# Second attention layer: values two visits behind the scores and placed right after them, weight transfers placed behind the first q transfers, scalings of V reordered

## The chip, the cores and the metric

The kernel runs on one core of one Trainium2 chip. The metric is device time in microseconds (us) of one execution; lower is better. Names of engines: PE is the matrix engine (PEld its weight loads), ACT the scalar engine, DVE the vector engine, POOL the GpSimd engine, SP the engine that issues most DMA transfers. A product, below, is a group of four matmuls (128 rows by 128 columns of weights, 512 moving columns) that adds into one PSUM bank.

## What is computed

Four residual steps on one input of 2048 tokens by 1024 features, in bf16: attention layer A, token-mixing MLP B, and both once more with the same weights.

```python
def _A_ref(x, wqkv, wo):
    H = 32; Dh = D // H
    W, dil = 8, 2
    qkv = (x @ wqkv) ...               # q, k, v: 32 heads of 32 features
    idx = pos[:, None] - off[None, :]  # each token sees itself and 7 more, every second one back
    ...
    logits = jnp.einsum("bhsd,bhswd->bhsw", q, kg) * scale
    attn = _softmax(where(mask, logits, -1e9))
    o = jnp.einsum("bhsw,bhswd->bhsd", attn, vg)
    return o @ wo                      # heads joined again

x = x + _A_ref(_layernorm(x), A_wqkv, A_wo)
x = x + _B_ref(_layernorm(x), ...)     # layernorm, matmul over tokens, gelu, matmul over tokens
x = x + _A_ref(_layernorm(x), A_wqkv, A_wo)
x = x + _B_ref(_layernorm(x), ...)
```

## The kernel before

Tokens are kept in two classes (even and odd positions), since the window steps by two; each class has 1024 tokens, eight tiles of 128. The first attention layer computes q and k by plain matmuls and goes through 32 **visits**; a visit is one group of four heads, one class, one half of that class's tokens. In a visit the scores S (`scores_mm`, L779) are matmuls with 32 weight columns each (128*32 in the profile's rows); ACT takes the exponential (`expo`, L794, two instructions e.a and e.b), DVE multiplies it by a band mask into the buffer `Pm` (`mask_r`, L809, four instructions m.0 to m.3), and later the values V (`values_mm`, L820) multiply `Pm` by v, again with 32 weight columns each, into one accumulator bank pair. Two ACT instructions make the reciprocal of the sums (l, `recip_a` L853; x, `recip_b` L856), and DVE multiplies by it (n, `divide` L859). `Pm` has room for three visits; a V of an odd visit also reads the end of the visit before it.

The second attention layer, the one that the change touches, computes v, q and k by seven half-size products in place of eight (sums and differences of the quarters of weights and of data). Class `Sevens` (L412) does this for v: ACT scales the four weight tiles to fp16 (`scale`), DVE forms the sums of weights (`t_sum`) and of data (`s_sum`); the scalings and the first sums are placed in the last round (i = 7) of the MLP's second matmul, `gemm2f` (L1453, its round starts at L1668). Class `QkBlocks` (L501) loads the eight blocks of q and k weights (`load`, two transfers ahead), scales them on ACT, forms their sums on DVE and stores both to DRAM (`keep`, two transfers of 512 KB a block). Class `Attention` (L529) then runs nine **cycles**, numbered p = 0 to 8. Cycle p makes k and q of one head group of one class by two times seven products (P1k to P7k, P1q to P7q), and holds the four visits of the group before it: scores S1 to S4 and values V1 to V4, with e, m, l, x, n of the same numbers. Cycle 0 has only products, cycle 8 only what is left of the seventh. Weights come back from DRAM by `load(phi)` (L565): two transfers of 512 KB, named Aq and Bq, for k (even phi = 2p) and q (odd phi = 2p+1). A q that is ready lies in the buffer `qs`; it has to be spread over the heads in `qB`, which the scores read, by DMA: d c11q, d y12q, d y22q, d c21q, four transfers of 32 KB each (L658), and a few columns by DVE (`hq`, L664).

The order on each engine is written out by hand in four strings (L531 to L534); "-" means of the cycle before:

```python
PE = "P1k P4q- P5k S1 P6k V1 P2k P7k S2 P3k V2 P4k P1q P5q S3 P6q V3 P2q P3q S4 P7q V4"
ACT = "abk c21q- e1a e1b pck l1 x1 Zk e2a e2b c11k l2 x2 c21k abq e3a e3b pcq l3 c11q x3 Zq e4a e4b l4 x4"
DVE = "m10 m11 m12 m13 n1 y22k y12k m20 m21 m22 n2 m23 t1 t2 m30 m31 m32 m33 n3 y12q y22q hq m40 ..."
SP = "dc21q- wk wq dc11q dy12q dy22q"
```

ab and pc copy a partial sum to another bank (L693), Z scales one (L696), c11 and c21 (L700), y12 and y22 (L701) write a finished quarter of k or q; t1 and t2 are sums of data for the other class, in cycles 0 to 3. P6 waits for ab, P7 and P3 for pc, P4 for y22. `wk` and `wq` load the weights of cycle p+1's q (phi = 2p+3) and of cycle p+2's k (phi = 2p+4); in cycle 0 these are loads 3 and 4. Each engine takes its instructions strictly in this order, SP too. The V of a visit stands one visit behind its S. After the cycles, four last visits are interleaved with the first output projections (L1913).

The queue of SP around the start of the attention is, in order: stores of blocks 4 and 5, load 1, stores of blocks 6 and 7 (L1891), load 2 (L1894), load 3 and load 4 (cycle 0), then twelve q transfers of cycle 0, then cycle 1's.

Of the kernel before, what the change touches and what calls it, by code (L numbers as in the profile page):

```python
# [9 lines left out]
ACT = mybir.ActivationFunctionType  # L10
# [18 lines left out]
def kernel(  # L29
# [498 lines left out]

    class Attention:  # L529
        NP = 4 * NG // 4  # L530
        PE = "P1k P4q- P5k S1 P6k V1 P2k P7k S2 P3k V2 P4k P1q P5q S3 P6q V3 P2q P3q S4 P7q V4"  # L531
        ACT = "abk c21q- e1a e1b pck l1 x1 Zk e2a e2b c11k l2 x2 c21k abq e3a e3b pcq l3 c11q x3 Zq e4a e4b l4 x4"
        DVE = ("m10 m11 m12 m13 n1 y22k y12k m20 m21 m22 n2 m23 t1 t2 m30 m31 m32 m33 n3 y12q y22q hq m40 m41 m42 n4 m43")
        SP = "dc21q- wk wq dc11q dy12q dy22q"  # L534

        def __init__(self):
            self.T = {}
# [42 lines left out]
        def needs(self, n, p):  # L580
            k, f = n[:-1], n[-1]
            o, d = ("q", p - 1) if f == "k" else ("k", p)
            if n[0] == "d":
                return [(n[1:], p)]
            if n[0] == "w":
                return [("P4q", p - 1)] if f == "k" else [("P4k", p)]
            if n == "hq":
                return [("y12q", p)]
            if f in "kq":
                r = {"P1": [("c11" + o, d)], "ab": [("P1" + f, p), ("y12" + o, d)], "P5": [("Z" + o, d)],  # L590
                     "Z": [("P5" + f, p), ("y22" + o, d), ("y12" + o, d)], "P6": [("ab" + f, p)],
                     "pc": [("P6" + f, p), ("c21" + o, d)], "P2": [("ab" + f, p)], "P7": [("pc" + f, p)], "P3": [("pc" + f, p)],
                     "c11": [("P2" + f, p)], "y22": [("P7" + f, p), ("Z" + f, p)], "y12": [("P3" + f, p), ("Z" + f, p)],
                     "P4": [("y22" + f, p)], "c21": [("P4" + f, p)]}[k]
                if f == "q" and k in ("c11", "y12", "y22", "c21"):
                    r.append(("d" + n, p - 1))
                if f == "k" and k == "P1":
                    r.append(("wk", p - 2))
                return r
            if n[0] == "t":  # L600
                return [("P5q", p)] if p == 3 else []
            c = n[1]
            o, d = {"1": ("4", p - 1), "2": ("1", p), "3": ("2", p), "4": ("3", p)}[c]
            return {"S": [("e" + o + "a", d), ("e" + o + "b", d), ("dc11q", p - 1), ("dy12q", p - 1), ("hq", p - 1)]
                    + ([("dc21q", p - 1), ("dy22q", p - 1)] if c in "34" else []),
                    "e": [("S" + c, p)], "m": [("e" + c + "a", p), ("e" + c + "b", p)],
                    "V": [("m" + o + str(r), d) for r in range(4)] + [("l" + o, d), ("n" + o, d)],
                    "l": [("V" + c, p)], "x": [("l" + c, p)], "n": [("x" + c, p)]}[n[0]]

        def there(self, n, p):  # L610
            if p < 0 or n[-1] in "kq" and n[0] != "w" and p >= self.NP:
                return False
            if n[0] == "w":
                return p < self.NP
            if n[0] == "t":
                return (n, p) in self.extra
            if n[0] in "SemVlxn":
                return 1 <= p <= self.NP - 1 + (0 if n[0] in "SemVlxn" else 1) and not (p == 1 and n[0] in "Vlxn" and n[1] == "1")
            return True

        def cycle(self, p):
# [29 lines left out]
        def do(self, n, p):  # L651
# [9 lines left out]
            if n == "hq":  # L661
                for h in range(HG):
                    hp = slice(h * DH, (h + 1) * DH)
                    r = nc.vector.tensor_copy(out=qB[0][hp, h, 512:512 + W], in_=self.qs[hp, 1, 0:W])  # L664
                return r
            if n[0] == "w":
                phi = 2 * p + (3 if f == "k" else 4)
                if phi < 2 * self.NP:
                    self.load(phi)
                elif phi - 2 * self.NP < NDC:  # L670
                    self.load_wo(phi - 2 * self.NP)
                return
# [29 lines left out]
                                                      op0=ALU.mult, op1=ALU.add)  # L702
            if n[0] == "t":
                return self.extra[n, p]()
            vis = 4 * (p - 1) + int(n[1]) - 1 - (n[0] in "Vlxn")
            u, b = divmod(vis, 2)
            if n[0] == "S":
                mm, x["ss", vis] = scores_mm(u, b)
# [744 lines left out]
    def gemm2f(g, src, dst, seam):  # L1453
# [214 lines left out]
        for i in range(2, NI):  # L1668
# [20 lines left out]
            if i == 2:  # L1689
                chain_(A, move, Z[:], pd)  # L1690
                scaled(j, q[j][:, 0], 1, 1)
            else:
                if more:
                    scaled(j, q[j][:, 0], 1, 1)
                else:
                    sv[0].scale(0)
                chain_(A, move, Z[:], pd)
                if more:
                    scaled(j, q[j][:, 1], 0, 1)
                else:  # L1700
# [7 lines left out]
            if i == 5:  # L1708
                power_wv()
            if not more:  # L1710
                sv[0].scale(1)
                sv[0].scale(3)
                for n in range(4):
                    for m in range(2):
                        sv[0].s_sum(m, n)
# [14 lines left out]
            else:  # L1730
                seam(i + 2 - NI)
            if not more:
                for m in range(2):
                    sv[0].t_sum(3, m)
                    sv[0].t_sum(1, m)
# [22 lines left out]
            in_order(product, pc, weights(A22), [T4k(k) for k in range(K)], False)  # L1758
            prev = pc
        i = NI - 1  # L1760
        quarter(i, 1, 0, prev)
        aggregate(i, 1)
        for m in range(2):
# [5 lines left out]

        return rest  # L1770

    sv = [None]
    NU = NG * DIL
    hT, qB = new_hT(), new_qB()
    for li in range(2):
# [75 lines left out]
            chain_("DVE", power, 0, 1 + NPRE, bc0[:].rearrange("p q b -> p b q"))  # L1851
            ahead_tiles = 4
        else:
            blocks, at = QkBlocks(), Attention()

            def ahead(p, n):
                two_ = (p, p + 1)
                if n == 0:
                    if p == 0:
                        rest()  # L1860
                        chain_("POOL", zero_p, nc.gpsimd)
                    elif p == 2:
                        chain_("POOL", zero_q, nc.gpsimd)
                    if p:
                        blocks.keep(p - 2)
                        blocks.keep(p - 1)
                    if p == 4:
                        at.load(0)
                elif n == 2:
                    for k in two_:  # L1870
                        blocks.scale(k)
                    if p == 6:
                        at.load(1)
                else:
                    if p + 2 < NI:
                        for m in range(4):
                            for k in range(2):
                                sv[0].s_sum(p + 2 + k, m)
                        for k in range(2):
                            blocks.load(p + 2 + k)  # L1880
                    for j in range(2):
                        for m in {2: (3,), 4: (1,), 6: (2, 4)}.get(p, ()):
                            chain_("DVE", at.t_sum, 0, m, j)
                    for k in two_:
                        blocks.sums(k)

            for k in range(2):
                blocks.load(k)
            sv[0].run(v, ahead)
            for k in range(2):  # L1890
# [12 lines left out]
            ahead_tiles = 7  # L1903
            plan = [1, 2, 2, 1, 1]
            k = 0
# [85 lines left out]
```

## Time and profile before

| | us |
|---|---|
| time of three runs, median (lowest, highest) | 1210.99 (1208.9, 1212.31) |
| profiled execution: its own time | 1207.65 |
| profiled execution: span from the first to the last instruction | 1205.6 |
| PE busy (99% of the span) | 1188.8 |
| DVE busy (67%) | 805.6 |
| ACT busy (61%) | 734.6 |
| last round of `gemm2f` on PE | 586.98 to 609.16 |
| `Sevens.run`, v | 609.16 to 658.04 |
| cycles 0 to 8 of the second attention | 658.04 to 798.67 |

Times in the trace count from the first instruction. A line of the timeline gives start, length, engine, line of the code, operation, what is written and read, shape, count, and in brackets the engine's idle time before it with what ended that. Since matmuls overlap in the array, the distance between two starts, not the length, is what a product costs: 0.863 us from one product to the next.

### The profile page before, as it was taken

The page shows a single profiled execution, that of the slowest core. Times are in us where ns is not written, and L with a number is a line of the kernel's source. Part 1 is how long each engine was busy: PE and PEld are TensorE (multiplying, and loading weights), DVE is VectorE, ACT ScalarE, POOL GpSimd, SP SyncE. Part 2 cuts the span into 40 slices and gives each one's busy share as a digit, 9 for nine tenths or more (in the row PEclk, how much of TensorE's full clock was granted, in tenths as well). Part 3 has the DMA queues.
Part 4 walks back from the last instruction along what each step waited for, and adds up shares of the span by engine and source line. Part 5 has one row for each costly group of instructions (what it writes and reads, how often), then busy time and mean ns, then how long its engine had stood idle before and what let it go on. Part 6 is the DMA issues. An engine that isn't in the chain of part 4 may idle for free.

```text
span 1205.6 us, 20706 instructions
## 1 busy us (share of the span) xinstructions
PE 1188.8 (99%) x7908; PEld 540.3 (45%) x7908; DVE 805.6 (67%) x1541; ACT 734.6 (61%) x1220; POOL 138.3 (11%) x124
## 2 busy tenths in 40 slices
PE   9999999999999999999999899999999999999998
PEld 4444444444444444444444344444444444444444
DVE  6558887887777546866678488789633422784663
ACT  4767876678878776665668488865443434432342
POOL 0000000281000041000040000002811212100000
PEclk9999999999999999999999899999999999999999
DMA  8922233696675778876468634544867755165520
GB/s 241 152 63 71 77 110 92 210 280 168 203 211 171 205 197 193 226 179 162 127 201 283 233 116 166 192 123 155 285 195 207 226 163 158 53 192 140 149 80 36
DMA packets 258739, 201.53 MB, mean 167 GB/s; under 512 B 50256, under 2 KB 228816, under 8 KB 255312
## 3 DMA queue, kind: packets, MB, share of 16 engines
q1 hardware_dynamic: 258640, 200.21, 57.6%
q8 instruction: 62, 1.02, 0.4%
q14 instruction: 37, 0.30, 0.1%
HBM read 147.07 MB, written 38.82 MB: 154 GB/s over the span
## 4 chain that ended last, share of the span: by engine, by line
PE 87%; DMA 4%; DVE 3%; ACT 3%; issue 1%; SPq 1%; DVEq 0%; ACTq 0%
PE s L1142 11%; PE m L750 9%; PE m L900 7%; PE m L1142 7%; PE s L1351 7%; PE a L1142 6%; PE s L1501 4%; PE m L1351 4%; PE m L642 4%; PE s L299 3%; PE a L1351 3%; PE m L1501 3%; PE s L642 3%; PE s L981 2%; PE s L1594 2%; PE s L787 2%
## 5 line engine op out<-in xcount | busy, mean ns | idle before, releaser
L811 DVE TENSOR_TENSOR Pm<-pc,band 32x640 bf16<-32x640 bf16 x256 | 124.2, 485 | 41.7 <-ACT pc L795 35.5
L1142 PEld LDWEIGHTS <-Sw 128*128 128x128 f16 x832 | 81.4, 98 | 98.9 <-issue 0.9
L750 PE MATMUL m<-hT,wqk 128*128 128x512 bf16 x512 | 115.9, 380 | 0.0
L900 PE MATMUL m<-wo,oT 128*128 128x512 bf16 x512 | 112.9, 379 | 1.2 <-DVE xn L907 1.1
L1142 PEld LDWEIGHTS <-w 128*128 128x128 f16 (+1 forms) x624 | 61.0, 98 | 73.6
L900 PEld LDWEIGHTS <-oT 128*128 128x128 bf16 x512 | 49.4, 98 | 61.8 <-issue 4.0
L795 ACT ACTIVATE pc<-s,shift 128x320 bf16<-128x320 f32 x128 | 60.7, 528 | 26.6 <-PE s L787 26.6
L750 PEld LDWEIGHTS <-wqk 128*128 128x128 bf16 x512 | 47.6, 98 | 59.0 <-issue 5.3
L995 POOL TENSOR_TENSOR T<-h 128x512 f16<-128x512 bf16 x16 | 18.4, 1153 | 442.6 <-ACT h L940 442.6
L995 DVE TENSOR_TENSOR py<-pz,m 128x512 f32<-128x512 f32 x14 | 9.6, 688 | 86.7 <-PE m L1142 64.7
L1142 PE MATMUL s<-T,Sw 128*128 128x512 f16 x288 | 66.2, 379 | 0.6 <-ACT s L1151 0.6
L995 POOL TENSOR_TENSOR Pm<-g 128x512 f16<-128x512 bf16 x24 | 28.6, 1210 | 286.0 <-ACT Pm L1076 163.9
L940 ACT ACTIVATE h<-xn,bi,rs 128x1024 bf16<-128x1024 bf16 x32 | 39.7, 1240 | 23.6 <-DVE bi L926 23.6
L1142 PE MATMUL m<-T,Sw 128*128 128x512 f16 x224 | 52.9, 379 | 0.0
L1142 PE MATMUL a<-h,w 128*128 128x512 bf16 x224 | 52.9, 379 | 0.0
L1118 ACT ACTIVATE w<-w,cs 128x2048 f16<-128x2048 bf16 x26 | 51.8, 1997 | 0.0
L907 DVE TENSOR_TENSOR xn<-m,xr 128x512 bf16<-128x512 f32 x64 | 43.9, 685 | 11.0 <-PE m L900 10.7
L1351 PEld LDWEIGHTS <-u 128*128 128x128 f16 x336 | 32.9, 98 | 39.6
L995 DVE TENSOR_TENSOR xs<-tq,xs 128x512 bf16<-128x512 f32 (+1 forms) x30 | 21.9, 731 | 42.7 <-ACT tq L1506 25.6
L862 DVE TENSOR_TENSOR oT<-a,rd 128x512 bf16<-128x512 f32 x64 | 44.2, 691 | 8.5 <-ACT rd L857 6.6
L1108 DVE TENSOR_REDUCE mx<-w 128x1 f32<-128x2048 bf16 x22 | 49.2, 2276 | 0.0
L995 DVE TENSOR_TENSOR py<-pz,s 128x512 f32<-128x512 f32 x12 | 8.3, 688 | 55.6 <-PE s L1142 46.6
(286 smaller groups left out, 2440.8 us busy)
## 6 DMA issues: line engine op xcount, KB each, us to landing
w<-in_B_w_dram SPq DMA_DIRECT2D x110, 512.0 KB, 6.0
sd<-Sw SPq DMA_DIRECT2D x13, 1024.0 KB, 7.9
Sw<-sd SPq DMA_DIRECT2D x13, 1024.0 KB, 5.1
xa<-xn SPq DMA_DIRECT2D x32, 256.0 KB, 4.0
xs<-xa SPq DMA_DIRECT2D x32, 256.0 KB, 3.3
Aq<-sdq SPq DMA_DIRECT2D x16, 512.0 KB, 6.0
Bq<-sdq SPq DMA_DIRECT2D x16, 512.0 KB, 4.7
Pm<-in_B_w_dram SPq DMA_DIRECT2D x26, 256.0 KB, 6.2
```

Source lines behind the costliest of these rows:

```text
L642: r = nc.tensor.matmul(out, lhsT=lhs[:, k, :], rhs=rhs[:, k, :], start=start and k == 0, stop=k == 3, skip_group_check=True)
L750: mm = nc.tensor.matmul(ps[:], lhsT=wts[part][:, kt, (g % 2) * P:(g % 2 + 1) * P], rhs=hT[:, kt, lo:lo + 512], start=(kt == 0), stop=(kt = ...
L795: return nc.scalar.activation(out=pc[:, 2 * n:2 * n + 2].rearrange("p t h k -> p (t h k)"), in_=ss[n][:, 0:2 * HG * GW], func=ACT.Exp, sca ...
L811: return nc.vector.tensor_tensor(out=Pm[rp, :, s0:s0 + HB, r * KG:r * KG + GW].rearrange("p h t k -> p t h k"), in0=pc[rp], in1=mk, op=ALU ...
L862: return nc.vector.tensor_tensor(out=oT[g][:, lo:lo + HB * P], in0=acc[0][:], in1=rd[:], op=ALU.mult)
L900: mm = nc.tensor.matmul(ps[:], lhsT=oT[g][:, cols(c, i)], rhs=wo[n][g // 4][:, g % 4, :], start=(g == 0), stop=(g == NG - 1))
L995: return eng.tensor_tensor(out=out, in0=a, in1=b, op=op)
L1108: return nc.vector.tensor_reduce(out=bx[fb][:, c:c + 1], in_=w1s[fb][c][:], op=ALU.max, axis=AX.XY, apply_absolute_value=True)
L1118: return nc.scalar.activation(out=w[:].bitcast(FP16), in_=w[:], func=ACT.Identity, scale=cs[:, fb + 1:fb + 2])
L1142: r = nc.tensor.matmul(out, lhsT=lhs[:, k, :], rhs=rhs[k], start=start and k == 0, stop=stop and k == NI - 1, skip_group_check=True)
L1351: r = nc.tensor.matmul(out, lhsT=lhs[k], rhs=rhs[k][:, cols_], start=start and k == 0, stop=k == K - 1, skip_group_check=True)
L1501: r = nc.tensor.matmul(out, lhsT=lhs[k], rhs=rhs[k], start=start and k == 0, stop=k == K - 1, skip_group_check=True)
```

## The change

- **Order of the cycles.** The V of a visit now stands two visits behind its S, and each V comes directly after the S of the same number. Since V of visit n-2 may read the part of `Pm` that the masks of visit n overwrite, these masks wait for that V. P1q moves ahead of P4k, P7q behind V4. ACT and DVE get new orders. Visit 26's values, which have no place in the cycles any more, follow right after them.
- **SP around the start.** Load 3 moves behind cycle 0's twelve q transfers. Load 4 and the stores of blocks 6 and 7 move into cycle 1, behind the transfers of c21q (`wx`, `late`). `wk` and `wq` begin with cycle 1.
- **Buffers.** Four of the eight output tiles `oT` are taken at cycle 0 and four at cycle 2.
- **First loads of q and k blocks.** The loads of blocks 0 and 1 stand ahead of the last store of `gemm2f` in SP's queue, not behind it.
- **Scalings of V.** In the last round of `gemm2f`, the order on ACT was tile 0, Z, tiles 2, 1, 3, move of the partial sum pc; it becomes Z, tiles 0, 2, 1, move, corner, tile 3. The sums of weights that need tile 3 follow it on DVE.

```diff
-        PE = "P1k P4q- P5k S1 P6k V1 P2k P7k S2 P3k V2 P4k P1q P5q S3 P6q V3 P2q P3q S4 P7q V4"
-        ACT = "abk c21q- e1a e1b pck l1 x1 Zk e2a e2b c11k l2 x2 c21k abq e3a e3b pcq l3 c11q x3 Zq e4a e4b l4 x4"
-        DVE = ("m10 m11 m12 m13 n1 y22k y12k m20 m21 m22 n2 m23 t1 t2 m30 m31 m32 m33 n3 y12q y22q hq m40 m41 m42 n4 m43")
-        SP = "dc21q- wk wq dc11q dy12q dy22q"
+        PE = "P1k P4q- P5k S1 V1 P6k P2k P7k S2 V2 P3k P1q P4k P5q S3 V3 P6q P2q P3q S4 V4 P7q"
+        ACT = "abk c21q- Zk e1a e1b l1 pck x1 e2a c11k l2 x2 abq e2b c21k e3a e3b l3 pcq x3 c11q Zq e4a l4 x4 e4b"
+        DVE = ("n1 y22k m10 m11 y12k m12 n2 m13 m20 t1 m21 m22 m23 n3 m30 m31 y12q y22q hq m32 n4 m33 m40 t2 m41 m42 m43")
+        SP = "dc21q- wx wk wq dc11q dy12q dy22q"
...
-                return [("P4q", p - 1)] if f == "k" else [("P4k", p)]
+                return {"x": [], "k": [("P4q", p - 1)], "q": [("P4k", p)]}[f]
...
+            if n[0] == "V":
+                j = (int(c) - 3) % 4
+                e = p - (c in "12")
+                return [(f"m{j + 1}{r}", e) for r in range(4)] + [("l" + o, d), ("n" + o, d)]
...
-                    "e": [("S" + c, p)], "m": [("e" + c + "a", p), ("e" + c + "b", p)],
-                    "V": [("m" + o + str(r), d) for r in range(4)] + [("l" + o, d), ("n" + o, d)],
+                    "e": [("S" + c, p)], "m": [("e" + c + "a", p), ("e" + c + "b", p), ("V" + c, p)],
...
-                return p < self.NP
+                return 1 <= p < self.NP and (n != "wx" or p == 1)
...
-            vis = 4 * (p - 1) + int(n[1]) - 1 - (n[0] in "Vlxn")
+            vis = 4 * (p - 1) + int(n[1]) - 1 - 2 * (n[0] in "Vlxn")
...
-                else:
-                    sv[0].scale(0)
                 chain_(A, move, Z[:], pd)
                 if more:
                     scaled(j, q[j][:, 1], 0, 1)
                 else:
-                    sv[0].scale(2)
+                    sv[0].scale(0)
...
             if not more:
+                sv[0].scale(2)
                 sv[0].scale(1)
-                sv[0].scale(3)
...
             corner(i, 0, 0, pa)
             corner_add(i, 0, 0)
+            if not more:
+                sv[0].scale(3)
+                sv[0].t_sum(3, 1)
+                sv[0].t_sum(1, 1)
...
             sv[0].run(v, ahead)
-            for k in range(2):
-                blocks.keep(6 + k)
-            oT = [gop.tile([P, S], BF16, name="oT", tag="go") for _ in range(NG)]
+            def late_():
+                at.load(4)
+                for k in range(2):
+                    blocks[0].keep(6 + k)
+
+            at.late = late_
+            oT = []
             at.start(v, oT, wo)
             at.load(2)
...
             for p in range(at.NP + 1):
+                if p in (0, 2):
+                    oT += [gop.tile([P, S], BF16, name="oT", tag="go") for _ in range(NG // 2)]
                 at.cycle(p)
+                if p == 0:
+                    at.load(3)
...
+            in_order(values, NU - 3, 0, v, oT)
+            chain_("DVE", norm.pop())
...
         def seam(n):
+            if n == 2:
+                blocks.append(QkBlocks())
+                for k in range(2):
+                    blocks[0].load(k)
```

More of the change, by code (lines that the diff above doesn't have):

```diff
@@ L596, in needs @@
                     r.append(("d" + n, p - 1))
-                if f == "k" and k == "P1":
-                    r.append(("wk", p - 2))
+                if k == "P1":
+                    r.append(("wq", p - 2) if f == "k" else ("wk", p - 1))
                 return r
@@ L617, in there @@
             if n[0] in "SemVlxn":
-                return 1 <= p <= self.NP - 1 + (0 if n[0] in "SemVlxn" else 1) and not (p == 1 and n[0] in "Vlxn" and n[1] == "1")
+                return 1 <= p < self.NP and not (p == 1 and n[0] in "Vlxn" and n[1] in "12")
             return True
@@ L665, in do @@
                 return r
+            if n == "wx":
+                self.late()
+                return
             if n[0] == "w":
@@ L1732, in gemm2f @@
             if not more:
-                for m in range(2):
-                    sv[0].t_sum(3, m)
-                    sv[0].t_sum(1, m)
+                sv[0].t_sum(3, 0)
+                sv[0].t_sum(1, 0)
             corner(i, 0, 0, pa)
             corner_add(i, 0, 0)
+            if not more:
+                sv[0].scale(3)
+                sv[0].t_sum(3, 1)
+                sv[0].t_sum(1, 1)
             if more:
@@ L1760, in gemm2f @@
         i = NI - 1
+        seam(2)
         quarter(i, 1, 0, prev)
@@ L1770, in gemm2f @@
         return rest
-    sv = [None]
+    sv, blocks = [None], []
     NU = NG * DIL
@@ L1853 @@
         else:
-            blocks, at = QkBlocks(), Attention()
+            at = Attention()
             def ahead(p, n):
@@ L1864, in ahead @@
                     if p:
-                        blocks.keep(p - 2)
-                        blocks.keep(p - 1)
+                        blocks[0].keep(p - 2)
+                        blocks[0].keep(p - 1)
                     if p == 4:
@@ L1870, in ahead @@
                     for k in two_:
-                        blocks.scale(k)
+                        blocks[0].scale(k)
                     if p == 6:
@@ L1879, in ahead @@
                         for k in range(2):
-                            blocks.load(p + 2 + k)
+                            blocks[0].load(p + 2 + k)
                     for j in range(2):
@@ L1884, in ahead @@
                     for k in two_:
-                        blocks.sums(k)
-            for k in range(2):
-                blocks.load(k)
+                        blocks[0].sums(k)
             sv[0].run(v, ahead)
-            for k in range(2):
-                blocks.keep(6 + k)
-            oT = [gop.tile([P, S], BF16, name="oT", tag="go") for _ in range(NG)]
+            def late_():
[4 more added lines that the diff above has]
+            oT = []
             at.start(v, oT, wo)
```

## The prediction

> **What bounds the kernel now.** I read the page first (PE busy nearly all of the span), then the list of PE's waits, then PE's and SP's timelines of the second attention.
>
> ```profile
> PE 1188.8 (99%) x7908; PEld 540.3 (45%) x7908; DVE 805.6 (67%) x1541; ACT 734.6 (61%) x1220; POOL 138.3 (11%) x124
> ```
>
> A change can therefore gain only by making PE's own work cheaper or by taking out one of its few waits. The largest, from the list of PE's waits (total, times, longest):
>
> ```profile
> PE s L787 <- DMA qB<-qs: 6.3, 5, 5.0
> ```
>
> The first scores of cycle 1 wait 5.0 us for q transfers; the other four waits make 1.3. PE's timeline (first attention, then the second):
>
> ```profile
> 101.56 3.63 PE L750 MATMUL m<-hT,wqk 128*128 128x512 bf16 x16
> 105.12 0.46 PE L787 MATMUL s<-qB,kT 128*32 128x160 bf16 x16
> 105.41 0.18 PE L832 MATMUL a<-Pm,v 128*32 128x8 bf16 x4
> ...
> 106.00 3.63 PE L750 MATMUL m<-hT,wqk 128*128 128x512 bf16 x16
> ...
> 671.70 1.03 PE L642 MATMUL s<-Tq,Bq 128*128 128x512 f16 x4
> 677.73 0.73 PE L787 MATMUL s<-qB,kT 128*32 128x160 bf16 x16 [5.00 <-DMA qB<-qs]
> 678.39 1.89 PE L642 MATMUL m<-Tq,Bq 128*128 128x512 f16 x4
> ...
> 687.31 1.03 PE L642 MATMUL s<-Tq,Bq 128*128 128x512 f16 x4
> 688.26 0.46 PE L787 MATMUL s<-qB,kT 128*32 128x160 bf16 x16
> 688.66 1.04 PE L642 MATMUL m<-Tq,Bq 128*128 128x512 f16 x4
> 689.62 0.19 PE L832 MATMUL a<-Pm,v 128*32 128x8 bf16 x4
> ...
> 690.23 1.04 PE L642 MATMUL s<-hT,Aq 128*128 128x512 bf16 x4
> ```
>
> See two things. After the wait, products take 1.89 in place of 1.03: the clock has fallen, which the windows show for 678 to 685 (granted clock 0.59; the clock's records say half speed from 676.87 for 6.83 us). And a switch from 128 to 32 weight columns costs about 0.1 each time, also between S and V when a product stands between them. SP's timeline shows why the q transfers were late:
>
> ```profile
> 661.83 0.39 SPq L526 DMA_DIRECT2D sdq<-Rq  x1
> 662.88 0.32 SPq L527 DMA_DIRECT2D sdq<-Sq  x1
> 663.29 1.04 SPq L569 DMA_DIRECT2D Aq<-sdq  x1
> 664.42 1.13 SPq L570 DMA_DIRECT2D Bq<-sdq  x1
> 665.65 0.41 SPq L569 DMA_DIRECT2D Aq<-sdq  x1
> 666.15 0.42 SPq L570 DMA_DIRECT2D Bq<-sdq  x1
> 666.66 0.49 SPq L569 DMA_DIRECT2D Aq<-sdq  x1
> 667.24 0.66 SPq L570 DMA_DIRECT2D Bq<-sdq  x1
> 668.83 13.65 SPq L658 DMA_DIRECT2D qB<-qs  x16
> ```
>
> Eight 512 KB transfers stand ahead. By the trace they land at 665.36, 667.14, 669.33, 670.62, 672.76, 674.05, 675.67 and about 676.9, and the first q transfer lands behind them, at 677.07: transfers of this queue land in the order of issue, A loads some 2.1 us after what is ahead, B loads and stores about 1.3. That is a queue in which work is moved, not removed.
>
> **The change, part by part.**
>
> *S and V side by side.* In the first attention they already stand so. Odd visit: the sixteen matmuls from 101.56 take 16 x 0.216 = 3.45, so S and V take 106.00 - 105.01 = 0.99. Apart, in the second: S 0.40 and its switch 688.26 - (687.31 + 0.863) = 0.09, V 0.61 and its switch 689.62 - (688.66 + 0.863) = 0.10: 1.20. The pair saves 0.21. In cycles 2 to 7 there are 24 pairs: -5.0.
>
> *New waits that take some back.* (a) y22q needs P7q, and P4q needs y22q: 0.21 until DVE starts (P3k's end to `kx` at 685.10), 0.75, and 0.05, so 1.01; V4 and P1k stood between, now only P1k with 0.86: 0.15 a cycle. (b) On ACT, Zk, both e1 and l1 now stand before pck: from P5k's end 0.20 + 0.60 + 0.43 + 0.43 + 0.63 + 0.55, and 0.11 to PE, make 2.95, where P7k would be reached after S1, V1, P6k and P2k in 0.50 + 0.56 + 1.73 = 2.79: 0.16. (c) Laying out DVE's new order with the rows' durations (masks 0.49, divisions 0.66, y 0.66, hq 0.7), the last mask of visit 3 ends 0.1 late for V1. About 0.4 a cycle, 2.2 by the end; bounds 1 and 4. The masks' wait for V costs nothing: V follows S at once, while e takes 0.86. DVE has 15.0 and ACT 14.3 us of work in the 17 us from 697 to 714, so a cycle of 16.5 still holds them, with little room.
>
> *The end.* P4q of cycle 7 loses V4's cover: 1.0 of waiting, not 0.54: +0.45. Visit 26's V, 0.68, moves behind the cycles: +0.68 there.
>
> *The scalings of V.* On ACT three scalings of 1.92 stood between Z (593.23) and the move of pc (599.40), and three stand there after: PE's wait of 0.86 at 600.09 stays. Tile 3's sums come 0.7 later on DVE, but the next stage waits for the POOL memset there until 613.2 anyhow. Blocks 0 and 1 load 0.7 earlier, which covers the wait of 0.38 at 625.24: -0.4. Bounds -1 and +0.7.
>
> *The queue of SP.* This decides. Cycle 0's twelve q transfers go out from about 668.5 with nothing ahead; four land by 672.2, S1 of cycle 1 is reached at about 672.4. So the wait of 5.0 and the slow clock go there; together they cost 684.02 - 672.56 - 3.58 = 7.9 (up to P3k, against two S and three products).
>
> What is late next: q transfers are issued 0.62 apart, so load 3 goes out after 12 x 0.62, at about 676.0, and its A lands 3.4 to 3.9 later (the shortest A landings), near 679.5. P1q of cycle 1, now ahead of P4k, needs it and is reached at 676.9: a new wait of 2.7. Then come four transfers of c21q, loads 4, stores of 6 and 7, load 5, load 6, and only then c11q, for which S1 of cycle 2 waits. These are ten transfers of 512 KB behind load 3's B (680.7). With A at 2.1 and the others at 1.3: 3 x 3.4 + 4 x 1.3 = 15.4; with 0.7 for each of the two groups of four q transfers, c11q has landed at 697.5. PE would be ready for S1 at 690.3 (P1q at 679.6, ten products to P5k, two pairs of S and V of 0.97, and (a)). So S1 of cycle 2 waits some 7 us, and the clock falls again. If every transfer took 1.29 it would be 695.0, if A took 2.6, 699. In the before kernel S1 of cycle 2 starts at 696.69. **The wait moves by one cycle, and the 7.9 us come back whole.**
>
> *The clock there.* Row: 5.0 us idle brought 5.97 us of work at half clock, 3.0 lost. I take 2.5, bounds 0 and 3.4.
>
> The Trainium skill (TensorE: Matmul & The Clock Gate, What's actually happening) states a free-running window of 3413 ns: one idle window halves the clock, one busy window gives it back. The 6.83 us of this trace are two such windows and agree. By this rule 2.7 us at P1q would leave the clock alone, some 7 us at S1 of cycle 2 would surely halve it, and the loss would be half of one to two windows, an estimate of 1.7 to 3.4, which would make the sum +1.2 to +2.9. It speaks against the change, since it charges the moved stall again.
>
> *Sum.* From S1 of cycle 2 to the first output projection (798.67) it took 101.98. After: -5.0 + 2.2 + 0.45 + 0.68, and 0.8 for the small waits on q transfers (1.3 now; cycles get shorter by 0.4, SP's sixteen issues don't; bounds 0 and 2.3), gives 101.1. With 697.5 + 101.1 + 2.5 = 801.1 against 798.67: +2.4; the scalings and loads -0.4: **+2.0**. The profiled execution took 1207.65 (its span 1205.6 and 2 around it), 3.3 under the median of the runs; the difference is put on the median: 1210.99 + 2.0 = **1213**. The forecast's own bounds: S1 of cycle 2 at 695.0 with no fall of the clock, -3.0; at 699 with 3.4 lost, +4.4. With the bounds of the new waits and of the small ones, about 1207 to 1217.
>
> **Rivals.**
>
> *The queue drains in time.* If stores run beside loads, so that the ten take under 8.2 us, S1 of cycle 2 starts at 690.3 and the clock stays: 690.3 + 101.1 - 0.4 - 798.67 = -7.7, so 1203; without P1q's wait 1200.6. For it: the queue is nearly empty from 662 to 676 and nothing of the order forces the q transfers of cycle 1 to be late but the weights ahead. Against: every landing of a backlog in this trace is 1.2 us or more behind the one before it, stores among loads too.
>
> *SP's queue becomes the pace* (slower). The first and the last of sixteen q issues stood 11.5 us apart at 708.89 (15 x 0.62 = 9.3, the rest stalls among them), the last landed 1.85 later, and S3 waited 0.16 at 722.37, in another cycle 0.85 at 757.10. From the first issue to S3 there were 13.5 us; three pairs less waiting leave 12.9. If c21q's transfers land later than that in every cycle, the cycles stay at 17.0 and the pairs give nothing: +2.8 more than forecast, and with 3.4 for the clock, +5.7: 1216.7. It decides as soon as the issues span over 11.0.
>
> *The order doesn't do what it says:* V waits for n of the V before, so that S and V don't touch. l, x, n take 0.63 + 0.62 + 0.69 plus gaps, about 2.2, and a V comes each 4 us, so hardly; it would give the same 1216.7 and shares that rival's chance.
>
> **How the numbers follow.** Forecast 0.5, drained queue 0.25, SP's pace 0.25. About 0.3% (3.6 us) is what a measurement of this kernel can tell from no change: faster 0.27 (the drained queue and a little of the forecast's low end), slower 0.35 (SP's pace and the forecast's upper fifth), same 0.38. The range from 1202 to 1219 leaves out less than 2 in 10.
>
> **What would show it.** Right: PE's waits list S1 of cycle 2 on `qB<-qs` with 4 us or more and a wait of P1q on `Aq` of 2 to 3; half clock after 695; S and V 0.95 to 1.0 together; the wait at 600.09 still there. Wrong: no wait at S1 of cycle 2, or landings of `sdq<-Rq` and `Sq` under 1 us apart; steady cycles of 17.0 (SP's pace) or under 16.2 (no new waits).

## The result, and the profile after

| | before | after |
|---|---|---|
| median of 22 runs (lowest, highest), us | 1209.24 (1206.34, 1212.31) | 1213.32 (1210.59, 1216.82) |
| profiled execution: own time, span | 1207.65, 1205.6 | 1213.54, 1211.6 |
| first product of `Sevens` to last output projection | 252.24 | 257.00 |
| S1 of cycle 2 to the first output projection | 101.98 | 105.56 |

The changed kernel is slower: ratio 1.0038, 95% interval 1.0028 to 1.0048, which is 4.6 us. In the changed kernel the lines named below stand three or six lines lower (scores L793 for L787, products L645 for L642, values L842 for L836, q transfers L661 for L658).

Of the 6.0 us between the two spans, 1.2 arise before the change's place: in the first MLP, between 399 and 416, one or two products wait for ACT for between 0.3 and 3.7 us in all, differently in each profile of this study, and in those of e6 and e8 half clock follows. So profiles are compared below by the stage from the first product of `Sevens` (609.16 before, 610.38 after) to the last output projection.

The first line of the page after has PE busy for less of a longer span. (The 134 matmuls fewer are records missing from the trace: the weight loads, PEld, are 7908 as before. A row of three matmuls in place of four, and 0.16 put down to `issue`, show such a place.)

```profile
PE 1177.5 (97%) x7774; PEld 543.4 (45%) x7908; DVE 806.3 (67%) x1541; ACT 732.5 (60%) x1220; POOL 138.5 (11%) x124
```

The list of PE's waits after (total, times, longest) says where PE stood still:

```profile
PE s L793 <- DMA qB<-qs: 8.1, 2, 6.2
PE s L645 <- DMA Aq<-sdq: 3.1, 1, 3.1
PE a L842 <- DVE Pm L817: 2.3, 3, 1.3
...
PE m L1507 <- ACT m L1512: 0.9, 1, 0.9
```

Where there was one wait of 5.0, there are waits of 3.1, 6.2 and 1.9 for transfers and one of 1.3 for masks. PE's timeline after gives their places:

```profile
676.95 0.81 PE L645 MATMUL m<-hT,Bq 128*128 128x512 bf16 x3 [0.16 <-issue]
680.84 1.89 PE L645 MATMUL s<-hT,Aq 128*128 128x512 bf16 x4 [3.08 <-DMA Aq<-sdq]
...
692.12 1.03 PE L645 MATMUL s<-Tq,Bq 128*128 128x512 f16 x4
699.30 0.72 PE L793 MATMUL s<-qB,kx 128*32 128x160 bf16 x16 [6.15 <-DMA qB<-qs]
...
708.69 1.03 PE L645 MATMUL s<-Tq,Bq 128*128 128x512 f16 x4
709.65 0.46 PE L793 MATMUL s<-qB,kx 128*32 128x160 bf16 x16
709.94 0.41 PE L842 MATMUL a<-Pm,v 128*32 128x136 bf16 x16
710.17 0.39 PE L846 MATMUL a<-Pm,ones 128*32 128x512 bf16 x4
710.39 0.18 PE L855 MATMUL a<-Pm,ones 128*32 128x24 bf16 x4
710.50 1.04 PE L645 MATMUL m<-Tq,Bq 128*128 128x512 f16 x4
```

P1q of cycle 1 waits at 680.84, S1 of cycle 2 at 699.30. The last five lines are a pair in a cycle without a wait: from 708.69 + 0.863 to 710.50 it costs 0.95, where S and V apart cost 1.20. SP's timeline after shows the cause of both waits:

```profile
669.35 7.51 SPq L661 DMA_DIRECT2D qB<-qs  x12
676.96 0.53 SPq L569 DMA_DIRECT2D Aq<-sdq  x1
677.59 0.38 SPq L570 DMA_DIRECT2D Bq<-sdq  x1
678.05 2.41 SPq L661 DMA_DIRECT2D qB<-qs  x4
680.57 0.53 SPq L569 DMA_DIRECT2D Aq<-sdq  x1
681.19 0.38 SPq L570 DMA_DIRECT2D Bq<-sdq  x1
681.62 0.42 SPq L526 DMA_DIRECT2D sdq<-Rq  x1
...
689.68 0.32 SPq L570 DMA_DIRECT2D Bq<-sdq  x1
690.05 10.16 SPq L661 DMA_DIRECT2D qB<-qs  x10
```

The first of twelve q transfers waits for its quarter of q until 669.35, and they go 0.63 apart. Load 2 had landed at 662.98; so this queue had no large transfer under way from then until 676.96, and the ten after load 3 land one behind the other from 685.20 to 698.42. The q transfers of line 690.05 land behind them, the fourth at 699.26, and S1 starts 0.04 later. The windows of PE's work (length; busy time of PE, PEld, DVE, ACT and POOL; granted clock; DMA share and GB/s) show the clock after the two waits, and after a third, of 1.95 at S3 of cycle 5:

```profile
676.91:680.32 3.41, 0.81 (x3) 0.20 (x2) 2.92 (x6) 0.90 (x2) 0.00 (x0) 1.00 0.69 241
680.32:683.73 3.41, 2.89 (x7) 1.04 (x8) 0.00 (x0) 0.96 (x2) 0.00 (x0) 0.50 0.91 248
693.97:697.39 3.42, 0.00 (x0) 0.00 (x0) 2.14 (x5) 0.00 (x0) 0.00 (x0) 1.00 0.93 337
697.39:700.80 3.41, 1.50 (x40) 1.12 (x40) 0.00 (x0) 0.95 (x2) 0.00 (x0) 0.50 0.13 34
700.80:704.21 3.41, 3.19 (x15) 1.19 (x9) 0.23 (x1) 1.71 (x3) 0.00 (x0) 0.50 0.21 58
```

```profile
758.83:762.24 3.41, 1.46 (x44) 0.97 (x44) 1.93 (x4) 1.03 (x3) 0.00 (x0) 1.00 0.67 208
762.24:765.65 3.41, 3.19 (x9) 1.22 (x8) 1.30 (x3) 2.34 (x5) 0.00 (x0) 0.50 1.02 395
```

Half clock (0.50) fills 13.65 us in four windows; before it filled 6.83. The third wait on PE, and what SP issued just before it:

```profile
760.84 0.46 PE L793 MATMUL s<-qB,kT 128*32 128x160 bf16 x16 [1.95 <-DMA qB<-qs]
```

```profile
755.24 1.53 SPq L895 DMA_DIRECT2D xr<-xb  x3
756.86 2.41 SPq L661 DMA_DIRECT2D qB<-qs  x4
```

The kernel before has the same three loads ahead of c21q's transfers in cycle 5, and its S3 waited 0.69 there.

### The profile page after: what moved, and what is told of

Same layout as the page of the kernel before. It is cut to its first block, busy times and chain, and to the rows that moved or that the text cites. A ratio compares the mean times of both kernels' runs of the same rounds, so it can differ in the third digit from the quotient of the medians.

```text
span 1211.6 us, 20545 instructions
## 1 busy us (share of the span) xinstructions
PE 1177.5 (97%) x7774; PEld 543.4 (45%) x7908; DVE 806.3 (67%) x1541; ACT 732.5 (60%) x1220; POOL 138.5 (11%) x124
## 4 chain that ended last, share of the span: by engine, by line
PE 87%; DMA 5%; DVE 3%; ACT 3%; issue 1%; SPq 0%; DVEq 0%; ACTq 0%
PE s L1148 11%; PE m L756 9%; PE m L906 7%; PE s L1357 7%; PE m L1148 7%; PE a L1148 6%; PE s L1507 4%; PE m L1357 4%; PE m L645 4%; PE s L299 3%; PE a L1357 3%; PE m L1507 3%; PE s L645 3%; PE s L987 2%; PE s L449 2%; PE s L1600 2%
## 5 line engine op out<-in xcount | busy, mean ns | idle before, releaser
L756 PE MATMUL m<-hT,wqk 128*128 128x512 bf16 x481 | 111.8, 379 | 3.1 <-issue 2.2
```

The costliest lines, as they stand in the source:

```text
L756: mm = nc.tensor.matmul(ps[:], lhsT=wts[part][:, kt, (g % 2) * P:(g % 2 + 1) * P], rhs=hT[:, kt, lo:lo + 512], start=(kt == 0), stop=(kt = ...
```

## The experiments

All kernels compute the whole of the reference. **Theory:** the queue of SP decides. The transfers that moved cost what the kernel lost, and the new orders bring about as much as they take. **Rival:** the orders cost the time (waits of V, the end, DVE with little room), and the queue is neutral, since one wait is taken out and one put in. Ratios are to the kernel before, with their 95% intervals; "stage" is the stretch named above, in the profile.

| run | ratio | stage, us |
|---|---|---|
| e1_order_alone | 1.0000 (0.9991 to 1.0009) | 251.19 |
| e2_queue_alone | 1.0038 (1.0024 to 1.0051) | 258.55 |
| e3_stores_back | 0.9979 (0.9970 to 0.9988) | 247.38 |
| e4_spread | 0.9992 (0.9980 to 1.0003) | 251.58 |
| e5_xr_late | 1.0041 (1.0027 to 1.0056) | 256.18 |
| e6_queue_and_xr | 0.9964 (0.9948 to 0.9980) | 246.91 |
| e7_and_end | 0.9984 (0.9973 to 0.9995) | 251.38 |
| e8_scalings_alone | 1.0002 (0.9988 to 1.0015) | 253.42 |
| e9_queue_best | 0.9943 (0.9922 to 0.9964) | 245.39 |
| e10_same_queue_old_orders | 0.9951 (0.9936 to 0.9967) | 245.08 |
| e11_end_filled | 0.9919 (0.9902 to 0.9937) | 242.71 |
| e12_queue_best_again | 0.9946 (0.9927 to 0.9965) | 244.27 |

### Orders alone, queue alone

e1 is the changed kernel with the queue of SP as it was; e2 is the kernel before with the new queue and the old orders, so that these lines go the other way round in it. Scalings and first block loads stay new in e1 and old in e2. The diff is that of e1 against the changed kernel:

```diff
-        SP = "dc21q- wx wk wq dc11q dy12q dy22q"
+        SP = "dc21q- wk wq dc11q dy12q dy22q"
...
-            at.late = late_
+            for k in range(2):
+                blocks[0].keep(6 + k)
...
-                if p == 0:
-                    at.load(3)
```

> The new orders of PE, ACT and DVE with SP's queue as before (stores 6 and 7, loads 2, 3, 4 ahead of cycle 0's q transfers). Theory (the moved transfers cost, the pairs of S and V gain): S1 of cycle 1 waits some 5 us again and the clock falls there (3 lost), P1q of cycle 1 and S1 of cycle 2 don't wait; against the changed kernel that is 8 us back and 13 us saved, so about 0.8 us under the kernel before (ratio 0.999, bounds 0.996 to 1.002). Rival (the orders cost by their own new waits, the queue is neutral): as slow as the changed kernel, +4 us, ratio 1.0035.

> The orders of PE, ACT and DVE as before, with SP's queue as changed (load 3 behind cycle 0's q transfers, load 4 and stores 6 and 7 in cycle 1). Theory: S1 of cycle 1 is free (7.9 us gained), P1q of cycle 1 waits 1 to 2 (it is reached later than in the changed order), S1 of cycle 2 waits 4 to 6 and the clock falls there: about +2 us against before, ratio 1.0016 (bounds 1.000 to 1.004). Rival (the orders cost, the queue is neutral or gains): ratio at or under 1.000, down to 0.994 if S1 of cycle 2 doesn't wait.

Measured: 1.0000 and 1.0038. The queue alone costs as much as the whole change; the orders, with the scalings and block loads, nothing. PE's waits in e1, then in e2:

```profile
PE s L793 <- DMA qB<-qs: 8.3, 6, 5.6
```

```profile
PE s L790 <- DMA qB<-qs: 10.9, 5, 8.0
```

e1 keeps the old wait at S1 of cycle 1 (5.6), e2 has it at S1 of cycle 2 (8.0, at 698.90), and the half clock there lasted 10.24 us in place of 6.83. So the theory holds and the rival falls. e2 lost more than was expected (1.0016, bounds 1.000 to 1.004): its wait was put at 4 to 6, and with 8.0 goes one window more of half clock.

### The stores alone put back

e3 leaves loads 3 and 4 where the change put them, and only the stores of blocks 6 and 7 go back ahead of load 2.

```diff
-            def late_():
-                at.load(4)
-                for k in range(2):
-                    blocks[0].keep(6 + k)
...
-            at.late = late_
+            at.late = lambda: at.load(4)
+            for k in range(2):
+                blocks[0].keep(6 + k)
```

> The changed kernel with the stores of blocks 6 and 7 alone put back to their old place ahead of load 2; loads 3 and 4 stay behind the q transfers. Theory: the four stores held the queue for 5.5 us of landings, so S1 of cycle 2 waits about 1 in place of 6.2 and its fall of the clock goes, P1q still waits 3: 7.5 us under the changed kernel, some 3.4 under before, ratio 0.997. Rival (the wait at S1 of cycle 2 comes from the loads of cycle 1, which stand closer in shorter cycles): S1 of cycle 2 still waits 4 or more, ratio 1.002 or more.

Measured 0.9979: under both kernels, where 0.997 was expected. PE's waits:

```profile
PE s L793 <- DMA qB<-qs: 4.5, 5, 2.2
PE s L645 <- DMA Aq<-sdq: 3.1, 2, 2.0
```

Four transfers fewer in the backlog shorten the wait at S1 of cycle 2 from 6.15 to 2.18, and the clock never falls. The four stores, 2 MB that SP could send from 662 on with nothing else under way, are what made the change a loss: with them back, the same change is a gain.

### Where else the loads can stand

e4 spreads the transfers: load 3 and the stores behind load 2, load 4 behind c11q's transfers of cycle 0, and in every cycle the load for the k after next (`wq`) behind c11q.

```diff
-        SP = "dc21q- wx wk wq dc11q dy12q dy22q"
+        SP = "dc21q- wk dc11q wx wq dy12q dy22q"
...
```

> The changed orders with another queue: load 3 and the stores of blocks 6 and 7 right behind load 2, ahead of cycle 0's q transfers, where the queue was empty; load 4 behind c11q's transfers of cycle 0; in every cycle the load for the k after next behind c11q's transfers, not ahead. Theory: no wait at P1q of cycle 1, none over 1 us at S1 of cycles 1 and 2, no fall of the clock before 755: 13 us under the changed kernel, 8 to 9 under before, ratio 0.993. Rival (the orders themselves cost): ratio 0.998 or more even with these waits gone. If the y12q transfers, now behind that load, come late, S2 waits up to 1 us a cycle, and the ratio is 0.997.

Measured 0.9992, a miss (0.993 expected, 0.997 if y12q came late): the early waits are gone, but the list of PE's waits now has thirteen small ones.

```profile
PE s L793 <- DMA qB<-qs: 10.9, 13, 1.7
```

They lie above all at S2 of every cycle (1.0 to 1.7 in five of seven) and at S3 of cycles 3 and 5: y12q and y22q now stand behind a load. The place of a load that is right in cycle 0 is wrong in the steady cycles. e5 takes up the wait at S3 of cycle 5 in the changed kernel. There SP issues the three loads of the residual (xr, 256 KB each, 755.24) just ahead of c21q's transfers (756.86); e5 moves them behind cycle 7.

```diff
-                if p == 4:
+                if p == 7:
                     todo[:] = order
                     for _ in range(3):
                         load_xr(res)
```

> The changed kernel with one move: the first three loads of the residual rows (xr, 256 KB each) go out after cycle 7 and not after cycle 4, where they stand ahead of c21q's transfers. Theory: the wait of S3 in cycle 5 (1.9 us) is theirs and goes, and with it the half clock from 762.24 (3.4 us at half speed, 1.7 lost): 3.6 us under the changed kernel, ratio to before about 1.001. Rival (SP's sixteen issues alone make S3 late): S3 of cycle 5 still waits over 1 us, ratio 1.003 or more.

Measured 1.0041, a miss (about 1.001 expected). The wait at S3 and the half clock at 762.24 are gone, but the first output projections now wait for an addition that needs xr. From S1 of cycle 2 to the first output projection this profile gains 2.5 us on the changed kernel's; the projections give 1.9 of it back:

```profile
PE m L906 <- DVE xn L913: 3.1, 3, 1.9
```

e6 joins both, but keeps the steady order and spreads in cycle 0 alone.

```diff
...
+     ("dc11q wx dy12q dy22q" if e == "SP" and p == 0 else getattr(self, e)).split()
...
+            at.load(3)
+            for k in range(2):
+                blocks[0].keep(6 + k)
+            at.late = lambda: at.load(4)
...
-                if p == 4:
+                if p == 7:
```

> The changed orders with the queue spread at the start only: load 3 and the stores of blocks 6 and 7 right behind load 2, load 4 behind c11q's transfers of cycle 0, the later cycles' order as in both kernels (loads ahead of c11q), and the xr loads after cycle 7. Theory: of the run with the stores back (2.5 under before) the waits of P1q of cycle 1 (2.0), P1k of cycle 1 (1.1), S1 of cycle 2 (2.2) and S3 of cycle 5 (1.6) go: 9 us under before, ratio 0.9925 (bounds 0.991 to 0.995). Rival (q transfers are late somewhere whatever the order, since each cycle moves 2 MB and sixteen q transfers): the waits on q stay over 4 us in total, ratio 0.997 or more.

Measured 0.9964, short of the expected 0.991 to 0.995. No wait for q is longer than 1.4 now, but they make 5.1 in all, over the 4 that the rival named; and the projection waits 2.4 for the addition that needs xr. e7 adds to e6 the first half of the first output projection ahead of cycle 7's last P4q, and the second half ahead of the values of visit 26.

```diff
+                if p == at.NP:
+                    half, add, store, ln = out_proj(*order[0], oT, wo, res, xa[li], h2)
+                    in_order(half, 0)
...
+            chain_("DVE", add, 0)
+            in_order(half, 1)
+            chain_("DVE", add, 1)
             in_order(values, NU - 3, 0, v, oT)
```

> As the run before, and the end of the cycles filled: the first half of the first output projection stands ahead of cycle 7's last P4q, the second half ahead of visit 26's values. Theory: the waits of P4q (0.8) and of visit 26's V (1.3) go: 2 us under the run before, ratio to before 0.991. Rival (the projection's banks or its addition on DVE take the place of these waits): same time as the run before.

Measured 0.9984, a miss (0.991 expected). A new wait takes the place of the old:

```profile
PE a L847 <- DVE oT L869: 4.6, 1, 4.6
```

The values of visit 27 need the division n of visit 26, and that came late; 4.6 us idle also brought half clock for 6.83 us. DVE's timeline of e7 says why: the additions stand ahead of that division, and they wait for xr, as in e5 and e6.

```profile
798.84 1.29 DVE L914 TENSOR_TENSOR xn<-m,xr 128x512 bf16<-128x512 f32 x2 [4.84 <-DMA xr<-xb]
800.05 0.68 DVE L869 TENSOR_TENSOR oT<-a,rd 128x512 bf16<-128x512 f32 x1
```

### The scalings alone

e8 is the kernel before with only the scalings of V and their sums reordered (Z, tiles 0, 2, 1, move, corner, tile 3, sums).

```diff
-                else:
-                    sv[0].scale(0)
...
-                    sv[0].scale(2)
+                    sv[0].scale(0)
...
+                sv[0].scale(2)
                 sv[0].scale(1)
-                sv[0].scale(3)
...
+            if not more:
+                sv[0].scale(3)
...
```

> The kernel before with the reordered scalings of V alone. Theory: three scalings stand before the move of pc as before, so PE's wait of 0.9 before the third last product group stays, nothing else moves: ratio 1.000 (0.999 to 1.001). Rival (tile 3's scaling, now after the corner, makes the first products of v late or frees 2 us on ACT): a new wait on the matmuls of the sevens, or the wait of 0.9 gone, ratio off by 0.001 either way.

Measured 1.0002, and PE's wait at 600 is there as before:

```profile
PE m L1501 <- ACT m L1506: 0.9, 1, 0.9
```

`Sevens` took 48.93 here and 48.89 before. That the stage of this profile is 1.2 longer than before's comes from elsewhere: S1 of cycle 7 waits 2.13 for q transfers and half clock follows for 3.41 us.

### The best queue, with the new and with the old orders

e9 has the new orders; load 3 and the stores stand behind load 2, load 4 behind the y12q transfers of cycle 0, in cycle 1 the load for the k after next behind c11q, and xr in cycle 7 behind the last load. e10 has the same queue with the strings of the kernel before on PE, ACT and DVE, and also its scalings and block loads.

```diff
-        SP = "dc21q- wx wk wq dc11q dy12q dy22q"
+        SP = "dc21q- wk wq dc11q dy12q dy22q"
+        SP0 = {0: "dc11q dy12q wx dy22q", 1: "dc21q- wk dc11q wq dy12q dy22q"}
...
```

> The changed orders with the queue once more: load 3 and the stores of blocks 6 and 7 right behind load 2; load 4 behind c11q's and y12q's transfers of cycle 0; in cycle 1 the load for the k after next behind c11q's transfers; the first xr loads in cycle 7 behind the last weights, ahead of its q transfers. Theory: the waits left on q transfers fall under 3 us in total, the first addition waits under 1, no fall of the clock within the attention; from cycle 0 to the last output projection some 195 us against 203.4 before and 198.4 in the run with queue and xr moved: ratio about 0.993 (bounds 0.991 to 0.996). Rival (waits on q move on again): still over 4 us of them, ratio 0.996 or more.

> The same queue as the run beside it, with the old orders of PE, ACT and DVE (V one visit behind, apart from S). Theory: without the late transfers the orders themselves differ by the prediction's terms: 5.0 saved by the pairs, 2.2 of new waits, 0.45 and 0.68 at the end, and 1.3 that visit 26's values waited, so this run is only about 0.4 us slower than the one beside it (bounds 1 faster to 2 slower), ratio to before near 0.993. Rival (the pairs gain more and the late transfers hid it): 3 us or more slower than the one beside it, ratio 0.996 or more.

Measured 0.9943 and 0.9951. Most of what was gained is the queue's, whichever the orders; the intervals of the two overlap. e9's waits for q make 2.8, under the 3 expected, but the clock fell once, which was not expected. e9's cycles 3 to 5 take 16.16 to 16.7 us and e10's 16.86 to 16.98. The end gives this back: from S1 of cycle 1 to S1 of cycle 7 e9 takes 100.18 and e10 101.95, from there to the last output projection e9 81.61 and e10 78.60. PE's timeline of e9 there:

```profile
790.78 1.02 PE L647 MATMUL m<-Tq,Aq 128*128 128x512 f16 x4 [0.84 <-DVE qs L711]
793.10 0.42 PE L846 MATMUL a<-Pm,v 128*32 128x136 bf16 x16 [1.29 <-DVE Pm L821]
```

P4q of cycle 7 waits 0.84 (0.54 in e10), the values of visit 26 wait 1.29, and half clock follows from 793.45 for 3.41 us. e11 fills this: the first half of the first output projection goes ahead of that P4q, visit 26's values behind it, then the second half. e12 is e9 once more.

```diff
             for p in range(at.NP + 1):
+                if p == at.NP:
+                    half, add, store, ln = out_proj(*order[0], oT, wo, res, xa[li], h2)
+                    in_order(half, 0)
...
             in_order(values, NU - 3, 0, v, oT)
+            chain_("DVE", add, 0)
+            in_order(half, 1)
             chain_("DVE", norm.pop())
+            chain_("DVE", add, 1)
```

> As e9_queue_best, with the end reordered: the first half of the first output projections ahead of cycle 7's last P4q, the values of visit 26 behind that half, the second half behind them, and then the four last visits. Theory (the end gives the pairs' gain back): in e9_queue_best P4q waited 0.8 there, the values of visit 26 waited 1.3 for their masks, and the clock fell at 793.45 for 3.41 us, 1.7 lost. Filled with work that waits for nothing, these go: 2 to 3.5 us under e9_queue_best, ratio to the kernel before about 0.992 (0.989 to 0.994), and no half clock between 785 and 800. Rival (as in e7_and_end, another wait takes their place: the values of visit 27 need the division of visit 26, which DVE reaches late): a wait of over 2 us of values for oT or n at the end, same as e9_queue_best or slower, ratio 0.994 to 0.997.

> e9_queue_best once more, beside e11_end_filled on the same chip. If its gain is the queue's and not the day's: ratio to the kernel before 0.992 to 0.997 again, about 1202 to 1204 where the kernel before runs 1208. If it was luck of one profile (the wait in the first MLP near 410 differs from run to run): 0.998 or more.

Measured 0.9919 and 0.9946. PE's timeline of e11 at the end:

```profile
789.75 1.89 PE L910 MATMUL m<-wo,oT 128*128 128x512 bf16 x7
791.47 1.03 PE L647 MATMUL m<-Tq,Aq 128*128 128x512 f16 x4
792.81 0.42 PE L846 MATMUL a<-Pm,v 128*32 128x136 bf16 x16 [0.31 <-DVE Pm L821]
```

P4q (791.47) waits no more, the values of visit 26 wait 0.31, no half clock is left there, and what e7 ran into (the values of visit 27 waiting for oT) is 0.20: in e11 the division stands ahead of the second addition, and xr, now issued ahead of cycle 7's q transfers, had landed by 790.60, so that no addition waits for it at 794.79 (DVE's first). The intervals of e11 and e12 overlap at one end (0.9927 to 0.9937), so the step from e9 to e11 is likely rather than sure; that e11 is under the kernel before, by 0.6 to 1.0%, is sure. Against e10 (0.9936 to 0.9967) it hardly overlaps, which speaks for the pairs once the end is filled; but the old orders with a filled end were not run, so what the pairs alone are worth is not shown.

## Why the prediction was right or wrong

- **The moved wait: right.** P1q waited 3.08 (2.7 forecast), S1 of cycle 2 waited 6.15 ("some 7"), of its 6.83 us of half clock 4.9 were work, so 2.45 were lost (2.5 forecast), and S1 of cycle 1 was free. From c21q's last landing the ten transfers took 698.42 - 683.08 = 15.3 where 15.4 was worked out. In before's time (1.22 less) c11q had landed at 698.0, forecast 697.5: +0.5, since load 3's second half landed at 681.2 and not at 680.7. e3 shows that the stores make up most of the wait.
- **S and V side by side: right.** A pair costs 0.95 in place of 1.20, so it saves 0.25 where 0.21 was worked out. Steady cycles took 16.28 to 16.4 with 16.5 forecast, 16.9 before: over six cycles about -0.8 against the forecast.
- **The end: half right.** P4q waited 0.84 (1.0 forecast). What the sum had as the bare 0.68 of moving visit 26's values also brought a wait of 1.3 for masks, which no step had: +1.3, the second term that was missing.
- **The small waits: right in length, wrong in what they cost.** They were put at 1.3 + 0.8; it became one of 1.95 at S3 of cycle 5, behind the xr loads. Since it lay nearly whole in one window of the clock, 1.7 us were lost at half clock on top. This step failed: the sum charged the clock for the large wait alone. In part it was chance, since a wait that falls into two windows need not cost this, as e9 and e12 show below. (The 0.85 that the working names at 757.10 counts from the end of the product before; the wait alone is 0.69 in the trace.)
- **The sum: right in sign, less than half in size.** +2.0 was forecast and +4.6 measured, within the forecast's own bounds (1207 to 1217 against 1210.99, so -4 to +6) but clear of no change, to which the forecast gave a little more chance (0.38) than to slower (0.35). From S1 of cycle 2 to the output projection 105.56 was measured and 101.1 + 2.5 = 103.6 forecast: +2.0, of which 1.7 + 1.3 - 0.8 make 2.2. S1 of cycle 2 started at 698.1 in before's time, where 697.5 less the 0.4 of scalings and loads was forecast: +1.0. The output projections took 0.2 less (62.73 to 62.52). So +2.0 becomes +4.8; the stage measured +4.8, the ratio +4.6. Split by experiments, the moved queue costs 5.8 in the stage with the new orders (257.00 against e1's 251.19) and 6.3 with the old ones, where the forecast's terms make 697.5 + 2.5 - 696.69 = 3.3; the rest of the change gains 1.1 (e1's stage against before's; the runs' times, at 1.0000 with 0.9991 to 1.0009, show hardly that much), where they make 1.3. The mechanism was the forecast's; the queue's cost was put too low.
- **The scalings and first loads: right.** The 0.86 was forecast to stay and stays (e8 1.0002). The wait of 0.38 at 625.24 is no longer listed, and `Sevens` takes 48.52 in place of 48.89, the -0.4 of the forecast. (The first record of cycle 0 is missing after; its start is taken as 659.76 - 0.863 from the next product.) But this 0.4 is waited away at S1 of cycle 2.
- **The rivals.** The queue did not drain in time: the four stores landed 0.9 to 2.1 behind what was ahead of them, none beside a load. SP did not become the pace: the steady cycles got shorter, to 16.28 to 16.4. S and V do touch.
- **The clock at P1q.** The rule of the Trainium skill (TensorE: Matmul & The Clock Gate, What's actually happening) was read so that a wait of 2.7 would leave the clock alone. The measured 3.08, of which 2.6 lay in one window, did not: half clock from 680.32 (1.45 us lost there). Here the measurement decides. It changed nothing of the time, since S1 of cycle 2 waits for landings that do not depend on it. At S1 of cycle 2 the rule's estimate of 1.7 to 3.4 holds the 2.45.

## What to carry to other kernels

A queue that is served in order loses its time for good when small transfers that wait for results stand ahead of large ones that wait for nothing: put what can go early into the stretch in which the queue is empty, and place a load by the cycle it is in, not by one rule for all. When work is packed tighter in the steady part, look at the last cycle too, for there the removed cover turns into waits. Charge for the clock by how much of one window a wait fills, and not by the length of the wait alone.

## What the runs showed of the hardware

**The clock falls after a window that is mostly idle, not only a wholly idle one.** In each profile all changes of the clock lie on one grid of 3.413 us. Cut on that grid, and without the last 5 us of each execution, thirteen windows at full clock had 2.03 us or more without PE work, six of them wholly idle, and half clock followed each; of two with 1.95 us, one was followed by it (the changed kernel's 758.83 above); of all those with 1.90 or less, none. At half clock the fourteen windows with at most 0.52 us idle brought full clock back, and the seven with 0.86 or more did not. The first line is e9's window with the waits of 0.84 and 1.29, of the thirteen the one with the least idle time (3.41 - 1.38 = 2.03). Behind it stand two after which the clock stayed: e3's, with a wait of 2.18 of which 1.90 lie in it, and that of the first-MLP wait of e10:

```profile
790.04:793.45 3.41, 1.38 (x24) 0.64 (x27) 3.28 (x9) 1.36 (x3) 0.00 (x0) 1.00 0.14 36
```

```profile
688.06:691.47 3.41, 1.51 (x8) 0.49 (x5) 3.29 (x7) 1.63 (x3) 0.00 (x0) 1.00 0.43 137
```

```profile
409.58:412.99 3.41, 1.46 (x8) 0.58 (x7) 3.31 (x10) 2.08 (x4) 0.00 (x0) 1.00 0.97 347
```

In the last two PE was busy for 1.51 and 1.46 of 3.41, as in the changed kernel's window at 758.83 (1.46), yet here the clock stayed. Busy time is modelled at a matmul's end, so a threshold finer than "between 1.9 and 2.03 us idle" can't be read. The place on the grid explains why the same waits (0.8 and 1.3 at the end) cost e9 half clock and the same program in e12 none: in e12 they fell into two windows, 0.91 and 1.39 idle. The Trainium skill (TensorE: Matmul & The Clock Gate, What's actually happening) states that one idle window of 3413 ns halves the clock: the traces agree on the length, and differ in that a window idle for 0.60 of it was enough.

**SP's queue looks as if it held eight transfers.** In the changed kernel, when the backlog is longest, an issue comes 0.01 to 0.06 us after the landing of the transfer eight ahead (q transfers issued at 691.71, 692.64, 693.94, 695.16; landings at 691.69, 692.62, 693.88, 695.15). The transfers signal eight semaphores in turn, so the one eight ahead is also the last to have used the same semaphore. Whether the program's waits on these semaphores or the queue itself does this was not tried.
